# The first k quad of an attention-plus-MLP kernel: loaded in f16 by GpSimd's casting DMA instead of an f32 load and a VectorE cast

## The chip, the core and the metric

The kernel runs on one core of one Trainium2 chip. The core has five engines that run side by side, each with its own list of instructions that it takes strictly in order: TensorE (PE in the profile, with its weight loads shown as PEld), VectorE (DVE), ScalarE (ACT), GpSimd (POOL) and SyncE (SP). [...] Transfers between HBM and the on-chip memory SBUF are done by 16 DMA engines; a DMA is issued from the list of one engine, here SP (queue q1 in the profile) or POOL (queue q0). Matrix products land in PSUM, which has eight banks, P0 to P7.

The metric is the device time in microseconds of one execution. Before the change the median of three runs is 365.93 us (365.68 to 366.21).

## The reference

Two stages. The first is an attention without softmax: for 8 batches and 12 heads, with 448 positions and a head size of 64,

```
scores = q @ k.T / sqrt(64)
attn   = max(scores, 0)**2 / 448
out    = attn @ v
```

The result, reshaped to 3584 tokens of 768 values, goes through two dense layers with a sigmoid GELU between them:

```
h = x @ w_in                              # 768 -> 2048
g = h / (1 + exp(-1.702 * h))
y = g @ w_out                             # 2048 -> 768
```

All inputs and the output are f32 in HBM. The kernel computes in f16 with f32 accumulation.

## The kernel before

**Tiles.** The attention is cut into 24 quads, numbered 0 to 23: one batch and four of its heads. For each quad there is a tile of q, of k and of v, each 128 partitions x 2 x 448 values. A quad's 448 keys are cut into 7 chunks j of 64. For a chunk, `scores` (line 143) makes four small products into two PSUM banks, one bank for each of the two head pairs a = 0 and 1. `relu` (line 156) copies one bank to SBUF through a max with 0, on ScalarE by default or on VectorE; `square` (line 165) squares a chunk; `attn_v` (line 173) multiplies with v. Before the scores, q and k have to be f16 and transposed. In the first quads this is done on TensorE: `trans_pe` (line 126) transposes into a PSUM bank with 14 small matmuls, and `trans_evac` (line 136) copies the bank to SBUF on VectorE. The dense layers then run over blocks of 384 and 512 tokens, as soon as the attention of those tokens is done.

**Two ways to load.** `load` (line 97) is an f32 DMA from SP into a staging tile, `kst` or `qst`, of which there is one each; `cast` (line 107) then makes the f16 tile on the engine that its word names. `load_cast` (line 102) is one DMA from POOL that reads f32 and writes f16. Both end in a tile of the pools `k16` and `q16`, two buffers each.

**What sets the order.** Nothing is planned at run time. A long list of words, written out by hand in line 468 and after, is turned into instructions one word after another, so each engine's list has the order of the words. The words that matter here, with u the quad:

- `jk`u, `jq`u: `load_cast` of k or q from POOL. `V`u: the same for v. `jwb2`: a part of w_in from POOL. `I`: the identity that the transposes need, made on POOL.
- `Lk`u, `Lq`u: `load` from SP. `K`u:d, `Q`u:a: the cast, on VectorE (d) or ScalarE (a).
- `z13@0 z1`: 14 matmuls of zeros on TensorE into bank P0.
- `tq`u@b, `tk`u@b: the transposes into bank b. `eq`u, `ek`u: their copies out of PSUM, on VectorE.
- `s`u.j@b.c: the scores of chunk j into banks b (a = 0) and c (a = 1). `r`u.j.a: the relu of one of the two banks, on ScalarE, or on VectorE with `:d`. `x`u.j: the square.

A bank is free again when the instruction that reads it is done. So a score waits for two readers, and TensorE, being in order, lets everything behind it wait too. The list begins like this (line 469; wrapped here):

```
jq1 z13@0 z1 jk1 I jwb2 Lq0 Q0:a tq0@1 Lk0 jq2 K0:d tk0@2 eq0 ek0 jk2 tq1@3 eq1
s0.2@4.5 s0.3@6.7 tk1@0 r0.2.1 V0 r0.3.0 r0.3.1:d ek1 r0.2.0 s0.5@1.2 r0.5.0
s0.1@3.5 r0.1.0:d s0.0@6.7 r0.0.0 r0.5.1:d r0.1.1 jk3 s0.4@0.4 s0.6@1.3 ...
```

Quad 0 alone has q and k loaded in f32 from SP; quads 1 to 5 use POOL's casting DMAs, and later quads use SP again with transposing DMAs.

Of the kernel before, what the change touches and what calls it, by code (L numbers as in the profile page):

```python
# [15 lines left out]
def kernel(  # L16
# [406 lines left out]
    with tc.manual_schedule():  # L423
# [35 lines left out]
        def zeros(e, p, n):  # L459
# [8 lines left out]
            "jq1 z13@0 z1 jk1 I jwb2 Lq0 Q0:a tq0@1 Lk0 jq2 K0:d tk0@2 eq0 ek0 jk2 tq1@3 eq1 "  # L468
            "s0.2@4.5 s0.3@6.7 tk1@0 r0.2.1 V0 r0.3.0 r0.3.1:d ek1 r0.2.0 s0.5@1.2 r0.5.0 s0.1@3.5 "
            "r0.1.0:d s0.0@6.7 r0.0.0 r0.5.1:d r0.1.1 jk3 s0.4@0.4 s0.6@1.3 r0.6.1:d r0.6.0 "  # L470
            "s1.0@6.2 r1.0.1 r1.0.0 r0.4.0 V1 r0.0.1:d s1.2@5.3 r0.4.1:d jq3 x0.6:a jwb0 r1.2.0 "
            "x0.5 s1.1@1.2 r1.1.1 x0.4 s1.5@6.0 r1.5.0:d x0.0 r1.5.1 jwa0 r1.2.1:d s1.3@7.4 x0.3 "
            "r1.1.0 x0.2 s1.4@5.2 x0.1:a tq2@6 x1.0 tk2@0 eq2 x1.5:a jk4 a0@3.1 ek2 r1.3.0 e0.1.0 "
            "jq4 s1.6@6.0 V2 jwa2 tk3@7 x1.1:a e0.0.0 r1.4.0 jwb1 r1.4.1:d ek3 s2.0@3.5 x1.4 "
            "e0.0.1:a tq3@2 jwa1 r1.3.1 x1.3 r2.0.1 jk5 s2.4@7.4 r1.6.0 r2.4.0 jq5 V3 e0.1.1 "
            "r2.4.1:d jwb3 s2.1@5.6 x1.2 r1.6.1 x1.6 s2.2@7.1 r2.0.0 a1@4.0 jwa3 r2.2.1 V4 r2.1.0 "
            "r2.2.0 r2.1.1 V5 x2.0 e1.0.0:a eq3 e1.1.0 s2.6@3.1 e1.0.1:a x2.1 jo1.0 r2.6.0 e1.1.1 "
            "s2.3@5.7 s2.5@6.2 r2.3.0 r2.3.1:d x2.2 r2.5.1 jo0.0 f0.3.0@4 f0.3.1 r2.6.1:d s3.3@3.0 "
            "s3.2@5.7 r3.2.1:d r3.3.1 r3.3.0 tk4@2 r2.5.0:d tq4@1 x2.3:a ek4 jo1.1 r3.2.0 x2.4 "
            "f0.2.0@7 x2.5:a x2.6 f0.2.1 s3.0@0.3 a2@6.2 r3.0.1 e2.0.1:a e2.1.0:a eq4 s3.1@5.3 "  # L480
            "r3.1.0 e2.1.1:a e2.0.0 jo0.1 r3.1.1:d x3.1 f0.1.0@1 f0.1.1 f0.1.2 x3.2 f0.3.2 r3.0.0 "
            "f0.2.2 g0.1 g0.3 v0.3:d f0.0.0@5 v0.1:d g0.2 s3.5@2.6 s3.6@3.0 r3.6.0 s3.4@1.4 r3.6.1 "
            "r3.4.1 r3.4.0:d f0.8.0@7 f0.8.1 f0.0.1 r3.5.1 r3.5.0:d f0.0.2 x3.4 v0.2 f0.8.2 "
            "s4.2@3.0 g0.0 r4.2.1:d x3.3:a s4.3@4.1 s4.1@6.2 r4.1.1 x3.5 r4.1.0 f0.6.0@5 f0.6.1 "
            "r4.3.0 x3.0 f0.6.2 g0.6 f0.4.0@0 f0.4.1 f0.4.2 g0.8 r4.3.1:d r4.2.0:d s4.4@2.6 "
            "r4.4.0:d tk5@4 x3.6 r4.4.1 tq5@5 g0.4 v0.4 s4.0@7.1 eq5:a ek5 s4.5@3.2 G3 a3@6.0 "
            "s5.6@5.4 r4.5.1 r4.0.0:d r4.5.0 x4.4 x4.2:a e3.0.0 s5.0@2.7 f0.7.0@3 r5.0.1:d r5.6.0:d "
            "r5.0.0 Lk6 f0.7.1 x4.1:a f0.10.0@6 r4.0.1 Lq6 f0.10.1 f0.10.2 g0.10 v0.10 f0.5.0@7 "
            "f0.5.1 f0.5.2 g0.5 K6:p e3.0.1:a Lk7 f0.7.2 f0.11.0@5 v0.6:d f0.11.1 r5.6.1 s5.1@2.1 "
            "r5.1.0 s4.6@6.7 f0.11.2 r5.1.1 f0.15.0@0 r4.6.0 v0.0:d x4.0 f0.15.1 x4.3 f0.15.2 g0.7 "  # L490
            "r4.6.1:d s5.4@4.2 x4.5 r5.4.1 x4.6 a4@1.6 r5.4.0:d s5.5@3.7 g0.11 s5.3@2.4 g0.15 "
            "e4.0.1:a s5.2@5.0 v0.15 r5.5.1:d x5.0:a f0.13.0@6 f0.13.1 f0.13.2 r5.5.0:d r5.3.0 x5.4 "
            "Rk6 x5.5:a V6 f0.9.0@7 S3.1 v0.8 e4.0.0 f0.9.1 r5.3.1 f0.14.0@3 v0.5 f1.4.0@2 f0.9.2 "
            "S3.2 f0.14.1 f0.14.2 g0.13 v0.7 V8 g0.9 r5.2.0:d f0.12.0@1 f0.12.1 S0.1 f0.12.2 V7 "
            "f1.1.0@4 v0.9 r5.2.1 v0.11 f1.4.1 f1.7.0@6 g0.14 v0.14 x5.2 f1.7.1 x5.3:a u1.3.0@7 "
            "x5.6 T1.1 x5.1:a a5@5.0 f1.1.1 g0.12 t1.3.0 Q6:d S1.1 e5.0.1:a u1.2.0@3 S2.1 Lq8 S2.2 "
            "f1.0.0@1 e5.0.0:a f1.1.2 S2.4 v0.12:d t1.2.0 f1.4.2 S1.2 T1.2 v0.13 S2.3 Rq6 g1.4 T1.4 "
            "A0.0.1@0 u1.2.1@0 b1.2.1 W0.1 f1.0.1 f1.3.0@5 f1.3.1 f1.3.2 W2.1 A0.0.3 f1.2.0@2 S3.3 "
            "u1.3.2 g1.1 g1.2.1 v1.1 f1.5.0@4 f1.5.1 v1.2.1 K7 f1.2.1 g1.3 f1.2.2 Lk8 W1.1 g1.2 "
            "f1.5.2 S3.4 A0.0.2@1 f1.7.2 g1.5 v1.2:d u1.2.2 v1.3 g1.7 f1.0.2 g1.0 v1.5 v1.4 t1.2.2 "  # L500
            "f1.6.0@5 t1.3.2 f1.6.1 T1.3 p0.0.0@2 W3.1 v1.0:d f1.6.2 u1.2.4 Q8:a t1.2.4 W0.2 u1.2.3 "
            "h0.0.0 v1.7:d W2.2 u1.3.4 W0.3 b1.2.3 g1.6 u1.2.5 W2.3 v1.6:d Lq7 g1.2.3 v1.2.3 "
            "s6.0@4.6 r6.0.0 W1.2 s6.2@1.5 u1.2.6 u1.3.1@4 r6.2.0:d Rk7 W3.2 b1.3.1 r6.0.1 Rq8 W3.3 "
            "W1.3 g1.2.5 s6.1@1.6 p0.0.1@3 r6.1.0 W0.4 t1.3.4 x6.0:a g1.3.1 u1.3.5 u1.3.3 r6.1.1:d "
            "l0.0.1 r6.2.1 p0.0.2 b1.2.6 x6.2:a b1.3.3 Q7:a Rq7 h0.0.2:d s6.5@1.6 r6.5.0:d r6.5.1 "
            "v1.3.1 s6.3@5.0 r6.3.1:d g1.3.5 K8:p x6.1:a v1.3.5 Lq9 Q9 u1.3.6 b1.3.6 g1.3.6 v1.3.6 "
            "Lk9 K9:p p0.0.4 h0.0.4 s6.4@1.6 r6.4.1 W3.4 r6.3.0 W2.4 r6.4.0 s6.6@0.7 r6.6.0 W1.4 "
            "A0.0.4 v1.2.5 p0.0.3 r6.6.1:d p0.0.5 x6.4 x6.5:a s7.2@4.6 l0.0.3 r7.2.0 r7.2.1 x6.3 "
            "Rk8 s7.0@5.1 r7.0.1:d r7.0.0 g1.2.6 l0.0.5 s7.1@0.7 r7.1.1:d p0.0.6 x6.6:a l0.0.6 Lq10 "
            "s7.3@4.6 A0.2.5@1 r7.1.0 r7.3.1 o0.1 r7.3.0:d a6@1.5 Lk11 e6.1.1 e6.1.0 e6.0.1:a "  # L510
            "s7.6@2.7 x7.2 r7.6.0 r7.6.1 Q10 e6.0.0:a s7.4@3.0 r7.4.0:d p1.0.0@6 s7.5@4.5 Rq9 "
            "r7.4.1 s8.1@2.7 r7.5.1 r8.1.0 s8.0@1.3 r8.0.1 x7.3 r7.5.0:d r8.0.0 x7.1:a Rk9 x7.6:a "
            "K11:p i0.2.0@0 s8.6@5.2 r8.6.0 x7.0 x7.5 r8.6.1 x8.6:a r8.1.1:d x7.4 n0.2.0 x8.1 "
            "a7@3.4 e7.1.0:a e7.0.0:a Lk10 Lq11 v1.2.6 s8.2@1.5 e7.1.1:a S1.4 s8.3@2.7 x8.0:a K10:p "
            "r8.2.0:d e7.0.1 A1.0.1@0 r8.2.1:d i0.2.1@0 r8.3.1 A1.0.3 r8.3.0 Rk11 A1.0.2@1 h1.0.0 "
            "n0.2.1:a p1.0.1@3 x8.3:a V9 o0.2 s8.4@1.4 s8.5@5.7 r8.4.0 r8.4.1 r8.5.1 x8.2 Q11 "
            "r8.5.0:d s9.2@2.0 Lk12 o0.0 V10 Rk10 r9.2.1:d V15 p1.0.2 x8.4 s9.1@1.4 r9.2.0 x8.5 "
            "s9.0@7.5 r9.1.0 a8@0.2 r9.1.1:d r9.0.0 s9.4@1.4 r9.0.1 s9.3@7.5 r9.3.1 l1.0.1 p1.0.3 "
            "e8.1.1:a u2.1.0@5 e8.0.1:a u2.0.0@2 S0.2 r9.3.0 S1.3 r9.4.1:d e8.0.0:a u2.1.1@7 t2.1.0 "
            "r9.4.0:d t2.0.0 T2.1 u2.2.0@4 e8.1.0 g1.3.3 T2.2 t2.2.0 T2.4 u2.0.2 T2.3 b2.1.1 "  # L520
            "u2.0.1@1 Lq12 g2.1.1 v1.3.3:d S0.3 u2.1.2 b2.0.1 u2.2.1@0 t2.0.2 t2.1.2 v2.1.1 g2.0.1 "
            "v2.0.1 u2.0.4 t2.0.4 A1.2.1@0 x9.1:a u2.1.4 u2.0.3 t2.1.4 u2.2.2 u2.1.3 S0.4 Rq11 "
            "b2.0.3 u2.0.6 g2.0.3 Rq10 b2.2.1 K12:p u2.0.5 b2.1.3 u2.1.6 g2.2.1 v2.2.1:d v2.0.3 "
            "g2.1.3 b2.0.6 u2.1.5 t2.2.2 v2.1.3:d Lk13 A1.0.4 u2.3.0@1 g2.0.5 b2.1.6 u2.2.4 "
            "t2.3.0:d g2.0.6 u2.3.1@2 g2.1.6 v2.0.5 b2.3.1 v2.0.6 u2.2.3 t2.2.4 g2.1.5 v2.1.6 "
            "g2.3.1 v2.1.5 b2.2.3 u2.3.2 t2.3.2 A1.2.2@1 x9.4:a h1.0.2:d u2.2.5 v2.3.1 u2.2.6 "
            "b2.2.6 u2.3.3 g2.2.5 Q12:a u2.3.4 p1.0.4 h1.0.4 v2.2.5 s9.5@7.5 g2.2.3 r9.5.0 g2.2.6 "
            "x9.3 t2.3.4:d s9.6@0.4 b2.3.3 u2.3.5 g2.3.5 u2.3.6 r9.5.1:d r9.6.1 K13:p p1.0.5 "
            "r9.6.0:d l1.0.3 Rk12 b2.3.6 x9.2 Lk15 l1.0.5 s10.3@7.1 r10.3.1 V13 K15:p s10.1@5.4 "
            "s10.0@0.2 r10.0.1 Rq12 p1.0.6 x9.6 r10.3.0:d r10.0.0 x10.0 r10.1.0 p1.2.0@6 r10.1.1:d "  # L530
            "x9.0:a l1.0.6 g2.3.6 h1.2.0 x9.5 s10.5@1.2 s11.1@7.0 r11.1.1 a9@5.4 r10.5.1 r10.5.0:d "
            "v2.2.6:d Lq14 o1.0 r11.1.0 A1.2.3 s10.2@3.0 s10.6@2.1 v2.3.5 r10.6.0 r10.2.0 r10.2.1 "
            "r10.6.1:d p1.2.1@7 e9.0.0 x10.3:a p1.2.2 s11.0@2.3 e9.0.1:a Q14 l1.2.1 o1.1 r11.0.1 "
            "s10.4@0.1 s11.3@5.4 x10.6 Lq13 A1.2.4 r11.0.0:d p1.2.3 r10.4.1 x10.1 h1.2.2 p1.2.4 "
            "r11.3.1 x10.5 r10.4.0 r11.3.0 x10.4 x10.2:a h1.2.4:d x11.3 l1.2.3 s11.2@3.2 x11.1 "
            "r11.2.0 r11.2.1 x11.2 Lk14 s12.2@1.4 v2.3.6 a10@0.5 s11.5@3.2 r12.2.0 r11.5.1 Rk13 "
            "Rq14 p1.2.6 e10.0.0 r12.2.1 x11.0:a r11.5.0:d l1.2.6 v2.2.3:d e10.0.1:a g2.3.3 "
# [133 lines left out]
```

## Time and profile before

| what | value |
|---|---|
| median of three runs | 365.93 us |
| the profiled execution's own time | 365.47 us |
| its span, first to last instruction | 363.7 us |
| TensorE busy | 355.3 us (98%) |
| VectorE busy | 309.6 us (85%) |
| ScalarE busy | 283.2 us (78%) |
| GpSimd busy | 123.4 us (34%) |
| moved by DMA | 51.39 MB |
| first scores of quad 0 start | 7.50 us |
| TensorE in the first 5 us | 3.84 us busy, all of it zeros |

The time is what the runs report; the span lies inside it, and the 1.8 us between the two are before the first and after the last instruction. A row of the timeline gives the start and the busy time in microseconds, the engine, the line, what is written from what, and how many instructions are merged in it; the brackets at the end tell how long the engine sat idle before and which work released it. A busy TensorE is not a TensorE at its peak, since the ends of matmuls are modelled.

### The profile page before, as it was taken

How to read it: one execution, taken by the hardware profiler on the slowest of the kernel's cores; microseconds unless marked ns; L12 is line 12 of the kernel's file. 1: busy time of each engine (PE TensorE's matmuls, PEld its weight loads, DVE VectorE, ACT ScalarE, POOL GpSimd, SP SyncE). 2: the span in 40 equal slices, each digit the busy share in tenths (PEclk: the TensorE clock that was granted, in tenths of full speed). 3: DMA queues.
4: the chain of work that ended last, by engine and by line, in shares of the span. 5: the costliest groups of instructions: out<-in, count | busy, mean ns of one | idle time of the engine just before them, and what ended most of it. 6: DMA issues, size and time to landing. Idle time of an engine off the chain costs nothing.

```text
span 363.7 us, 9020 instructions
## 1 busy us (share of the span) xinstructions
PE 355.3 (98%) x3562; PEld 231.8 (64%) x3562; DVE 309.6 (85%) x577; ACT 283.2 (78%) x550; POOL 123.4 (34%) x171
## 2 busy tenths in 40 slices
PE   8899999999999999999999999999999999999995
PEld 4445555655579555885569655787558755687763
DVE  3998999799899998988999799978897999775672
ACT  3998995799989888988997899588996598362410
POOL 5655174425526240254243251145202221021300
PEclk9999999999999999999999999999999999999999
DMA  8999999959898789458995599515590031110315
GB/s 193 188 205 205 238 230 203 203 57 268 178 219 171 136 254 172 135 103 187 195 193 114 126 186 213 133 51 104 99 198 8 1 88 43 45 45 2 87 36 141
DMA packets 65227, 51.39 MB, mean 141 GB/s; under 512 B 35744, under 2 KB 61856, under 8 KB 65184
## 3 DMA queue, kind: packets, MB, share of 16 engines
q1 hardware_dynamic: 48256, 36.32, 42.3%
q0 software_dynamic: 16608, 14.09, 26.1%
q8 instruction: 28, 0.46, 0.5%
q10 hardware_dynamic: 320, 0.39, 0.3%
q14 instruction: 15, 0.12, 0.1%
HBM read 45.61 MB, written 11.01 MB: 156 GB/s over the span
## 4 chain that ended last, share of the span: by engine, by line
PE 87%; ACT 5%; DVE 5%; DMA 1%; issue 1%; SPq 0%; ACTq 0%
PE ox L203 29%; PE hx L203 29%; PE sc L150 9%; PE av L181 8%; PE ht L228 7%; PE os L203 4%; ACT at L163 3%; DVE at L161 1%; DMA kst<-in_k_dram 1%; ACT at L169 1%; DVE at L88 1%; ACT xe L79 1%; DVE asum L88 1%; PE tr L131 1%; DVE xe L83 0%
## 5 line engine op out<-in xcount | busy, mean ns | idle before, releaser
L163 ACT ACTIVATE at<-sc 128x448 f16<-128x448 f32 x228 | 111.5, 574 | 13.6 <-PE sc L150 12.2
L169 ACT ACTIVATE at<-at 128x896 f16<-128x896 f16 x72 | 68.6, 967 | 0.4
L161 DVE TENSOR_SCALAR at<-sc 128x448 f16<-128x448 f32 x108 | 64.4, 615 | 5.1 <-PE sc L150 4.6
L88 DVE TENSOR_TENSOR at<-at 128x896 f16<-128x896 f16 x96 | 61.4, 657 | 3.2 <-ACT at L163 2.7
L203 PEld LDWEIGHTS <-win 128*128 128x128 f16 x624 | 56.7, 98 | 8.6 <-issue 2.4
L217 POOL TENSOR_SCALAR go<-gf 128x512 f16<-128x512 f32 x48 | 35.9, 747 | 71.2 <-ACT gf L214 57.5
L88 DVE TENSOR_TENSOR gf<-hx,gf 128x512 f32<-128x512 f32 (+1 forms) x78 | 47.7, 624 | 14.3 <-PE hx L203 9.6
L214 ACT ACTIVATE gf<-gf 128x512 f32<-128x512 f32 (+1 forms) x78 | 44.5, 581 | 15.2 <-DVE gf L88 15.0
L150 PE MATMUL sc<-qT,kT 64*64 64x448 f16 x672 | 51.7, 359 | 1.7 <-ACT at L163 0.7
L217 POOL TENSOR_SCALAR ge<-gf 128x384 f16<-128x384 f32 x47 | 29.4, 626 | 65.7 <-ACT gf L214 63.7
L203 PE MATMUL ox<-wout,go 128*128 128x384 f16 x256 | 46.1, 326 | 0.0
L203 PEld LDWEIGHTS <-winS 128*128 128x128 f16 x468 | 42.5, 98 | 5.5 <-issue 1.6
L203 PEld LDWEIGHTS <-go 128*128 128x128 f16 x320 | 30.1, 98 | 22.4 <-issue 4.8
L181 PE MATMUL av<-at,v 64*64 64x448 f16 x672 | 36.6, 350 | 0.3
L203 PE MATMUL hx<-T,winS 128*128 128x256 f16 (+1 forms) x312 | 36.8, 260 | 0.0
L203 PEld LDWEIGHTS <-ge 128*128 128x128 f16 x256 | 24.2, 98 | 17.4 <-issue 3.4
L150 PEld LDWEIGHTS <-kT 64*64 64x64 f16 x672 | 18.0, 105 | 26.8 <-issue 21.5
L203 PE MATMUL ox<-wT,asum 128*128 128x384 f16 x192 | 34.9, 326 | 0.0
L79 ACT ACTIVATE gf<-hx 128x512 f32<-128x512 f32 (+1 forms) x50 | 26.3, 542 | 11.0 <-PE hx L203 7.6
L203 PE MATMUL hx<-xo,win 128*128 128x256 f16 x252 | 32.1, 273 | 0.0
L203 PEld LDWEIGHTS <-asum 128*128 128x128 f16 x224 | 21.2, 98 | 16.1 <-issue 2.3
L181 PEld LDWEIGHTS <-v 64*64 64x64 f16 x672 | 20.5, 107 | 11.9 <-issue 2.1
(77 smaller groups left out, 472.7 us busy)
## 6 DMA issues: line engine op xcount, KB each, us to landing
out_dram<-osb SPq DMA_DIRECT2D x52, 192.0 KB, 3.1
qst<-in_q_dram SPq DMA_DIRECT2D x19, 448.0 KB, 4.1
kst<-in_k_dram SPq DMA_DIRECT2D x19, 448.0 KB, 5.0
v<-in_v_dram POOLq DMA_DIRECT2D x24, 224.0 KB, 6.3
win<-in_moe_w_in_dram POOLq DMA_DIRECT2D x8, 384.0 KB, 10.7
wout<-in_moe_w_out_dram POOLq DMA_DIRECT2D x4, 768.0 KB, 22.3
q<-in_q_dram POOLq DMA_DIRECT2D x5, 224.0 KB, 7.6
k<-in_k_dram POOLq DMA_DIRECT2D x5, 224.0 KB, 6.7
```

The costliest lines, as they stand in the source:

```text
L79: nc.scalar.activation(out=o, in_=i, func=AF.Copy)
L88: eng[e].tensor_tensor(out=o, in0=x, in1=y, op=op)
L131: nc.tensor.matmul(out=ps[64 * a:64 * a + 64, j * 128:(j + 1) * 128], lhsT=x[:, a, 64 * j:64 * j + 64], rhs=ident[:, :], is_transpose=True)
L150: nc.tensor.matmul(out=sc[a][c, 0:S], lhsT=st["kT"][r, j, c], rhs=st["qT"][r, :, c], start=True, stop=True)
L161: nc.vector.tensor_scalar(out=o, in0=i, scalar1=0.0, scalar2=None, op0=ALU.max)
L163: nc.scalar.activation(out=o, in_=i, func=AF.Relu)
L169: nc.scalar.activation(out=at, in_=at, func=AF.Square)
L181: nc.tensor.matmul(out=av[s][64 * a:64 * a + 64, 0:S], lhsT=v16[r, a, 64 * j:64 * j + 64], rhs=at[r, a, :], start=(j == 0), stop=(j == J - 1))
L203: nc.tensor.matmul(out=o, lhsT=lhs(i), rhs=rhs(i), start=start and i == 0, stop=i == n - 1, skip_group_check=True)
L214: nc.scalar.activation(out=o, in_=i, func=AF.Gelu_apprx_sigmoid, scale=1.0 / SC)
L217: eng[e].tensor_scalar(out=o, in0=i, scalar1=SC, scalar2=1.0, op0=ALU.mult, op1=ALU.mult)
L228: nc.tensor.matmul(out=hp[g, f][:, 0:n], lhsT=w[:, i, fo:fo + 128], rhs=xts[g][:, i, 0:n], start=i == 0, stop=i == NK - 1)
```

## The change

Quad 0's k no longer comes as `Lk0` and `K0:d`. It comes as `jk0`, a casting DMA, and that is the first instruction that POOL issues. The list of words is also put in another order in its first stretch; after `r0.2.0` it is the same, word for word, to its end.

```diff
-jq1 z13@0 z1 jk1 I jwb2 Lq0 Q0:a tq0@1 Lk0 jq2 K0:d tk0@2 eq0 ek0 jk2
-tq1@3 eq1 s0.2@4.5 s0.3@6.7 tk1@0 r0.2.1 V0 r0.3.0 r0.3.1:d ek1 r0.2.0
+jk0 jq1 z13@0 z1 I jk1 jwb2 Lq0 Q0:a tq0@1 jq2 tk0@2 eq0 ek0 jk2
+s0.2@4.5 s0.3@6.7 r0.2.1 tq1@3 tk1@0 V0 r0.3.0 r0.3.1:d eq1 ek1 r0.2.0
 s0.5@1.2 r0.5.0 s0.1@3.5 r0.1.0:d s0.0@6.7 r0.0.0 r0.5.1:d r0.1.1 jk3 ...
```

Engine by engine:

- POOL: before jq1, jk1, I, jwb2, jq2, jk2; after jk0, jq1, I, jk1, jwb2, jq2, jk2. One DMA more, and jk1 behind the identity.
- SP: before Lq0, Lk0; after Lq0 alone. The next k load from SP is Lk6, much later.
- VectorE: before K0, eq0, ek0, eq1, r0.3.1, ek1, r0.1.0; after eq0, ek0, r0.3.1, eq1, ek1, r0.1.0. The cast is gone, and eq1 stands behind r0.3.1.
- TensorE: before tq0, tk0, tq1, s0.2, s0.3, tk1, s0.5; after tq0, tk0, s0.2, s0.3, tq1, tk1, s0.5.
- ScalarE: the same.

The functions are untouched: `load_cast` was there for quads 1 to 5, and its k and q take turns in the same two buffers as before.

## The prediction

> **What bounds the kernel now.** I read the shares of busy time first: TensorE 98%, so over most of the span TensorE sets the time. But the change touches none of that work: the list is the same after `r0.2.0`. So it can only move the moment at which the rest begins. The chain of work that ended last begins with the load of quad 0's k, to 5.49 us, then its cast, its transposes, the copy of kT, the first scores, and from 7.93 us ScalarE's relus. That stretch in the timeline (start, busy us, engine, line, work; in brackets the idle time before, and what ended it):
>
> ```profile
> 4.31 0.95 ACT L79 ACTIVATE q<-qst 128x896 f16<-128x896 f32 x1 [2.07 <-DMA qst<-in_q_dram]
> 5.31 0.58 PE L131 MATMUL tr<-ident,q 128*64 128x128 f16 x14
> 5.51 0.63 DVE L83 CAST k<-kst 128x896 f16<-128x896 f32 x1 [4.41 <-DMA kst<-in_k_dram]
> 6.06 0.62 DVE L83 COPY qT<-tr 128x896 f16<-128x896 f16 x1
> 6.19 0.58 PE L131 MATMUL tr<-ident,k 128*64 128x128 f16 x14 [0.30 <-DVE k L83]
> 6.45 0.71 POOL L104 DMA_DIRECT2D q<-in_q_dram  x1 [2.36 <-DVE k L83]
> 6.61 0.56 PE L131 MATMUL tr<-ident,q 128*64 128x128 f16 x14
> 6.82 0.62 DVE L83 COPY kT<-tr 128x896 f16<-128x896 f16 x1
> 7.36 0.61 DVE L83 COPY qT<-tr 128x896 f16<-128x896 f16 x1
> 7.50 0.57 PE L150 MATMUL sc<-qT,kT 64*64 64x448 f16 x8 [0.33 <-DVE kT L83]
> 7.93 4.47 ACT L163 ACTIVATE at<-sc 128x448 f16<-128x448 f32 x10 [2.67 <-PE sc L150]
> 8.00 0.58 PE L131 MATMUL tr<-ident,k 128*64 128x128 f16 x14
> 8.15 0.62 DVE L161 TENSOR_SCALAR at<-sc 128x448 f16<-128x448 f32 x1 [0.17 <-PE sc L150]
> 8.51 4.51 PE L150 MATMUL sc<-qT,kT 64*64 64x448 f16 x40
> 8.69 0.61 DVE L83 COPY kT<-tr 128x896 f16<-128x896 f16 x1
> 9.22 2.80 DVE L161 TENSOR_SCALAR at<-sc 128x448 f16<-128x448 f32 x5
> ```
>
> Two things to see. The cast stands on the way to the first scores, and holds back the copy of qT too, which was ready when tq0 ended at 5.89. And once ScalarE starts at 7.93 it runs without a gap. The busy times by stretch (columns: stretch, length, then busy us of PE, PEld, DVE, ACT, POOL, with counts, clock, DMA share, GB/s) say how long that lasts:
>
> ```profile
> 10.00:12.50 2.50, 2.26 (x21) 0.78 (x20) 2.50 (x6) 2.50 (x7) 2.34 (x4) 1.00 1.18 158
> 12.50:15.00 2.50, 1.71 (x31) 0.84 (x32) 2.50 (x6) 2.50 (x6) 0.00 (x0) 1.00 1.23 191
> 15.00:20.00 5.00, 4.81 (x85) 2.70 (x80) 5.00 (x11) 5.00 (x10) 4.14 (x6) 1.00 1.25 205
> ```
>
> DVE and ACT are both full to 20 us. TensorE waits for none of its transfers between 14 and 60 us, and is 100% busy from 35 us. So a shift of both engines' streams at 10 us should reach the end nearly whole.
>
> Last, the DMA queues in slices of 0.2 us, at 4.4, 4.6 and 4.8 us (packets, MB, share of 16 engines):
>
> ```profile
> q1 hardware_dynamic: 45, 0.08, 104.1%
> ...
> q1 hardware_dynamic: 45, 0.08, 98.0%
> q0 software_dynamic: 3, 0.00, 8.2%
> ...
> q0 software_dynamic: 36, 0.03, 98.6%
> q1 hardware_dynamic: 21, 0.02, 24.2%
> ```
>
> POOL's first transfer, jq1, was issued at 1.25 us, yet q0 moves nothing until q1, with q and k of quad 0, runs dry.
>
> [...] Here SP's first DMA moved packets 1.1 us after its issue, and a lone v load at 246.0 us moved its first at 1.4 us and landed at 3.7[...]. [...] jq2, which needs tq0 (over at 5.89), began at 6.45, 0.31 after the cast's end at 6.14. [...] the longest new idle time below is 0.85 us, so I leave the clock alone.
>
> **The change part by part.** Two groups: the new load, and the new order.
>
> *Is jk0 in time?* It takes jq1's place: issued at 1.25, first packet not before 2.65 (1.25 + 1.4). Before, q1 carried 512 packets to 5.0 us at 225 a us. Now it carries q's 256, which end at about 3.7. Then jk0's 256 packets at q0's rate (47 in 0.2 us, 235 a us) take 1.1 us, to 4.8; jq1 itself took 1.7 us from its first packet (4.75) to landing (6.45), so jk0 should land at about 5.4. It is needed when tq0 has gone through: tq0 starts at 5.31 as before (it waits for ScalarE's cast of q and the end of the zeros), and a following set of transposes enters 0.42 later (6.19 to 6.61): 5.73. In time by 0.3. jq1 then lands at 6.5, as before. jk1, now issued after the identity at about 3.5, is ready by 4.9, before the engines reach it at 5.9, and lands at 7.65 as before (2.15 + 5.5). Total packets are the same, so the rest of the queue is unmoved. [...]
>
> *SP* loses one issue of 0.45 us, with nothing behind it until Lk6 at 37.94: nothing. *POOL* gains one issue of 0.7 us in a stretch where it then sat idle 2.36 us before jq2: nothing. Its buffer waits stay the same kind: jk2 waits for tk0 as before, jk3 for tk1, which ends at 8.66 instead of 8.58.
>
> *The first scores.* tk0 5.73, ends 6.31 (+0.58). VectorE: eq0 at 5.94 (5.89 + 0.05), ek0 0.54 later (6.82 to 7.36) at 6.48, done 7.10. s0.2 at 7.16 (before 7.50): **0.34 us gained**. The cast of 0.63 yields no more, because the path of q sets the start now, and the two copies stand one behind the other.
>
> *What the order does with it.* s0.3 is 0.21 behind (8.51 to 8.72, the second four of that row) at 7.37. tq1 follows s0.2 by 0.50 (7.50 to 8.00 before, for tk1): 7.66, done 8.24. tk1 8.08, done 8.66. s0.5 follows by 0.51: 8.59 (before 8.51). VectorE sits idle from 7.10 to 7.81, when s0.3 is there (7.37 + 0.44), where before it did eq1. Then r0.3.1 at 7.81, eq1 at 8.35 to 8.97 (before 7.36 to 7.97), ek1 to 9.50. Now s0.1 needs bank P3, which eq1 empties: 9.02, before 8.72. Behind it in TensorE's order, s0.0 goes at 9.23, before 8.96. Relus come 0.43 after their scores:
>
> - ScalarE: r0.2.1 at 7.59 (0.34 early), two more at 0.42 each, r0.5.0 at 9.02 (s0.5; 0.20 early), r0.0.0 at 9.66 (before 9.64). The gain is gone.
> - VectorE: r0.1.0 at 9.45 (before 9.22), r0.5.1 at 9.98, done 10.59 (before 10.36).
> - s1.0's second bank is P2, freed by r0.5.1: 10.64, before 10.42. r1.0.1 on ScalarE then at 11.07; its own turn would be 9.66 + 3 x 0.42 = 10.92, and it was 10.91 before. **0.16 us lost**.
>
> Sum: -0.34 to the first scores, +0.50 by the later eq1 and what stands behind it: +0.16 from 11 us on, with VectorE at about +0.2. Both run full after that, so nothing gives it back before 20 us, and I find no slack that surely does later. The profiled execution would take 365.47 + 0.16 = 365.63. The median shown is 0.46 above that execution, so by the median 365.93 + 0.16 = **366.1 us**, which is no change: 0.2% of the time is 0.73 us, about what a measurement of this kernel can tell from none.
>
> **Rivals.**
>
> *The gain is kept.* If eq1 doesn't delay s0.1 (had VectorE a faster way to it, or the relus more slack than the 0.43 I use), ScalarE keeps its 0.34: 365.6. For it: ScalarE's first wait of 2.67 us is the chain. Against it: 0.71 us of new idle time on VectorE.
>
> *Absorbed.* Between 20 and 30 us VectorE is idle for 1.3 us and ScalarE for 0.6, so that a late stream can catch up there if TensorE isn't waiting for it just then: 365.9. Against it: TensorE also waits for both in that stretch (0.26 us for VectorE at 23.78).
>
> *jk0 is late, and the kernel slower.* If q0's first packet at 4.75 was not queueing but the start-up of POOL's first DMA (3.5 us after its issue), jk0 lands where jq1 did, at 6.45. tk0 starts at 6.5, kT is ready at 7.7, s0.2 goes at 7.79, 0.63 later than above, and all behind it: 0.16 + 0.63 = +0.8, 366.7. It begins to cost when jk0 lands after 5.7, and passes 0.2% at a landing of about 6.4. For it: the trace has no other first DMA. Against it: 1.4 us for a lone v load, and each slice shows q0 taking up what q1 leaves.
>
> *The change doesn't do what it says* is not among them: the cast and the f32 load are gone from the lists.
>
> **How the numbers follow.** Forecast 0.55; gain kept 0.17; absorbed 0.13; jk0 late 0.15. Only the last stands at the 0.2% line (366.66), and gets 0.10 beyond it; shifts that reappear larger in a later stage, which I can't work out, add 0.06 to slower and 0.08 to faster. So faster 0.08, same 0.76, slower 0.16. The range goes from the kept gain with 0.3 for the scatter of runs (365.3) to the late jk0 with 0.3 (367.0). The forecast alone: 365.8 to 366.5.
>
> **What would show it.** Right: s0.2 at about 7.16 and tk0 right behind tq0; r0.2.1 at 7.6, but r0.0.0 near 9.66 and r1.0.1 near 11.07; eq1 at 8.35 and idle time before r0.3.1 on VectorE; q0's packets from 3.7 us. Wrong: TensorE idle before tk0 with a DMA as the releaser (jk0 late), q's landing later than 4.3 (the two queues mix after all), a wait for jk1 before tk1, or the streams apart at 20 us by something other than +0.2.

## The result, and the profile after

The changed kernel takes 368.25 us (median of 4 runs, 367.94 to 369.15) where the kernel before takes 366.07 (4 runs, 365.68 to 366.63): a ratio of 1.0062, 95% interval 1.0040 to 1.0085. It is slower by about 2 us, where 366.1 and no change were forecast. The profiled execution took 367.94 us, with a span of 366.2 against 363.7.

The same stretch of the timeline as before the change (start, busy us, engine, line, work; in brackets the idle time before, and what ended it):

```profile
4.31 0.95 ACT L79 ACTIVATE q<-qst 128x896 f16<-128x896 f32 x1 [2.08 <-DMA qst<-in_q_dram]
5.74 0.87 PE L131 MATMUL tr<-ident,q 128*64 128x128 f16 x14
6.54 0.58 PE L131 MATMUL tr<-ident,k 128*64 128x128 f16 x14
6.66 0.62 DVE L83 COPY qT<-tr 128x896 f16<-128x896 f16 x1 [5.56 <-PE tr L131]
7.20 0.61 DVE L83 COPY kT<-tr 128x896 f16<-128x896 f16 x1
7.87 0.57 PE L150 MATMUL sc<-qT,kT 64*64 64x448 f16 x8 [0.74 <-DVE kT L83]
8.37 0.58 PE L131 MATMUL tr<-ident,q 128*64 128x128 f16 x14
8.52 0.62 DVE L161 TENSOR_SCALAR at<-sc 128x448 f16<-128x448 f32 x1 [0.70 <-PE sc L150]
9.06 0.61 DVE L83 COPY qT<-tr 128x896 f16<-128x896 f16 x1
```

The cast is gone, and VectorE idles 0.70 us before r0.3.1, as worked out. But the first scores start at 7.87, not at 7.16. In this execution TensorE was slow for longer: the 14 zeros took 4.66 us in place of 4.21, so tq0 started at 5.74 in place of 5.31, and its 14 transposes took 0.87 us in place of 0.58. That hides how late k is, which landed at 6.50; the experiments show it bare. The busy times by stretch (stretch, length, busy us of PE, PEld, DVE, ACT, POOL with counts, clock, DMA share, GB/s) say that VectorE and ScalarE are full again from 10 us on:

```profile
10.00:12.50 2.50, 2.14 (x28) 0.78 (x21) 2.50 (x6) 2.50 (x6) 2.50 (x4) 1.00 1.15 160
15.00:20.00 5.00, 4.71 (x95) 3.07 (x94) 5.00 (x12) 5.00 (x10) 3.47 (x6) 1.00 1.26 204
```

To see where the rest went, each instruction is matched with the same one of the kernel before, and their starts are subtracted. The table gives the shift in us against the profiled execution before: of ScalarE's first relu, of ScalarE's instructions at 10 to 11 us, and the middle one of all instructions in a later stretch. The tail is a length, from the start of VectorE's last instruction to the end of the span:

| execution | first relu | ScalarE at 10-11 us | 25-88 us | from 104 us | from 287 us | tail | span |
|---|---|---|---|---|---|---|---|
| kernel before | 0 | 0 | 0 | 0 | 0 | 4.04 | 363.7 |
| changed kernel | +0.37 | +0.75 | +0.81 | +1.48 | +1.24 | 5.27 | 366.2 |

So there are two losses in the changed kernel: 0.8 at the start, and 1.23 in the last 5 us, where the list of words is the same. The step near 100 us is scatter: in the twelve later profiles it lies between -0.5 and +0.7, mostly near +0.6, and it is +0.6 in the second profile of the kernel before, whose first profile was on the fast side there. The tail is not: in the profiles below it is 4.03 to 4.06 with the old load, as long as VectorE has no instruction fewer, and 5.24 to 5.50 with the new load, as long as nothing is added in its place.

The closing waits of SyncE say what the tail waits for (engine, line, what it waited for: us in total, times, longest). In the kernel before:

```profile
SPq L666 <- DMA out_dram<-osb: 1.4, 2, 0.9
```

In the changed kernel:

```profile
SPq L665 <- DMA out_dram<-osb: 2.4, 3, 1.7
```

It waits for the output transfers, and longer. The DMA queues around the last outputs (packets, MB, share of 16 engines), first before, in the 1.0 us from 358.0, 1.65 us ahead of VectorE's last instruction:

```profile
q1 hardware_dynamic: 44, 0.05, 19.2%
q14 instruction: 1, 0.01, 2.8%
```

Then after, in the 1.0 us from 362.6, 1.71 us behind the start of that instruction, and in the 0.8 us behind it:

```profile
q1 hardware_dynamic: 77, 0.10, 42.8%
q10 hardware_dynamic: 75, 0.09, 25.9%
q14 instruction: 1, 0.01, 4.7%
...
q1 hardware_dynamic: 3, 0.00, 2.8%
q10 hardware_dynamic: 5, 0.01, 2.1%
```

One packet of 8 KB of instructions (0.047 x 16 x 1.0 = 0.75 us on one DMA engine) has moved from ahead of the last outputs into the midst of them. The packet runs from 1.87 to 2.62 us behind the start of VectorE's last instruction. Nearly all outputs are through by 2.63; four data packets of SP's queue (q1) and four of ScalarE's (q10) follow one behind the other from 2.62 to 3.32, by their spacing one engine's share (an estimate). Before, nothing comes after 2.63. The late share starts where the instruction packet ends in the other executions too: at 2.59 behind a packet that ends at 2.60 in the changed kernel repeated, and at 2.66 behind 2.67 in its third execution.

### The profile page after: what moved, and what is told of

Its sections match the earlier page's. It is cut to its first block, busy times and chain, and to the rows that moved or that the text cites. A ratio compares the mean times of both kernels' runs of the same rounds, so it can differ in the third digit from the quotient of the medians.

```text
span 366.2 us, 9018 instructions
## 1 busy us (share of the span) xinstructions
PE 355.8 (97%) x3562; PEld 232.1 (63%) x3562; DVE 309.9 (85%) x576; ACT 284.1 (78%) x550; POOL 123.8 (34%) x172
## 4 chain that ended last, share of the span: by engine, by line
PE 89%; DVE 5%; ACT 4%; issue 1%
PE hx L203 29%; PE ox L203 29%; PE sc L150 9%; PE av L181 7%; PE ht L228 7%; PE os L203 5%; ACT at L163 3%; DVE at L161 1%; PE zp L463 1%; DVE at L88 1%; PE tr L131 1%; DVE asum L88 1%; ACT at L169 1%; ACT xe L79 1%; DVE osb L396 0%
## 5 line engine op out<-in xcount | busy, mean ns | idle before, releaser
L88 DVE TENSOR_TENSOR at<-at 128x896 f16<-128x896 f16 x96 | 62.7, 671 | 3.4 <-ACT at L163 2.7
L214 ACT ACTIVATE gf<-gf 128x512 f32<-128x512 f32 (+1 forms) x78 | 44.6, 583 | 14.9 <-DVE gf L88 14.7
```

The costliest lines, as they stand in the source:

```text
L88: eng[e].tensor_tensor(out=o, in0=x, in1=y, op=op)
L214: nc.scalar.activation(out=o, in_=i, func=AF.Gelu_apprx_sigmoid, scale=1.0 / SC)
```

## The experiments

### Which part costs what: four kernels on one chip

*The changed kernel again, and the kernel before again*, unedited.

> The changed kernel once more, for a second profile. In the first one it lost 0.37 us up to the first scores [...], 0.5 by 20 us from the later eq1, 0.67 at 98 to 102 us where VectorE's additions met GpSimd's casts, and about 1.2 after the last output DMA was issued. Theory ORDER (only the later eq1 belongs to the change, the rest is scatter of single executions): the same 0.5 between first scores and 20 us, but the other three terms differ from the first profile; the ratio to before over the rounds is about 1.001 to 1.002. Theory SYSTEMATIC (all of it belongs to the change): ratio about 1.006, first scores again near 7.87 us, and the same loss at 98 to 102 us.

> The kernel before, unchanged, for a second profile. ORDER: first scores may lie anywhere between 7.5 and 8.2 us[...]; VectorE's two long additions at 98 to 101 us vary in length. SYSTEMATIC: first scores at 7.50, r0.0.0 at 9.64, the span 363.7 within 0.3. Ratio 1.000 in both.

*The load alone*: the casting load first on POOL, the rest of the list in its old order.

```diff
-jq1 z13@0 z1 jk1 I jwb2 Lq0 Q0:a tq0@1 Lk0 jq2 K0:d tk0@2 eq0 ek0 jk2
+jk0 jq1 z13@0 z1 I jk1 jwb2 Lq0 Q0:a tq0@1 jq2 tk0@2 eq0 ek0 jk2
 tq1@3 eq1 s0.2@4.5 s0.3@6.7 tk1@0 r0.2.1 V0 r0.3.0 r0.3.1:d ek1 r0.2.0
```

> The new load alone: jk0 first in POOL's queue and no f32 load or cast of k, but the old order of tq1, eq1 and the scores. ORDER: first scores 0.34 us earlier than before at the same clock, the relus all 0.3 earlier, ratio about 0.999. SYSTEMATIC, with the load as its cause [...]: ratio about 1.003 to 1.006, first scores near 7.9.

*The order alone*: the f32 load and the cast as before, the new order behind them.

```diff
 jq1 z13@0 z1 jk1 I jwb2 Lq0 Q0:a tq0@1 Lk0 jq2 K0:d tk0@2 eq0 ek0 jk2
-tq1@3 eq1 s0.2@4.5 s0.3@6.7 tk1@0 r0.2.1 V0 r0.3.0 r0.3.1:d ek1 r0.2.0
+s0.2@4.5 s0.3@6.7 r0.2.1 tq1@3 tk1@0 V0 r0.3.0 r0.3.1:d eq1 ek1 r0.2.0
```

> The new order alone: tq1 behind the first scores and eq1 behind r0.3.1, with the old f32 load and cast of quad 0's k. ORDER: first scores at 7.50 as before, r0.0.0 and r0.1.0 then 0.4 to 0.6 later than before, ratio about 1.0015. SYSTEMATIC with the order as its cause [...]: ratio about 1.004 to 1.006.

Measured, with the kernel before at 366.36 us (37 runs):

| kernel | us | ratio, 95% interval | first relu | ScalarE at 10-11 us | 25-88 us | from 104 us | from 287 us | tail |
|---|---|---|---|---|---|---|---|---|
| changed, again | 367.94 | 1.0036, 1.0020-1.0052 | +0.49 | +1.09 | +1.13 | +0.81 | +0.56 | 5.38 |
| before, again | 366.36 | 0.9999, 0.9986-1.0012 | +0.03 | +0.04 | +0.08 | +0.67 | +0.67 | 4.04 |
| load alone | 368.12 | 1.0040, 1.0025-1.0054 | +0.73 | +0.80 | +1.57 | +2.27 | +2.07 | 5.26 |
| order alone | 366.69 | 1.0006, 0.9994-1.0018 | +0.02 | +0.40 | +0.44 | +1.03 | +1.03 | 4.06 |

Neither theory holds as a whole: the repeated changed kernel loses again at the start and in the tail (SYSTEMATIC), but not near 100 us, where only scatter is seen (ORDER). By the times, the load carries the loss, and the order alone can't be told from no change. Within its execution the order costs 0.42 (+0.02 at the first relu, +0.44 from 25 us on), at the place that was worked out. Its timeline:

```profile
7.52 0.57 PE L150 MATMUL sc<-qT,kT 64*64 64x448 f16 x8 [0.72 <-DVE kT L83]
8.17 0.62 DVE L161 TENSOR_SCALAR at<-sc 128x448 f16<-128x448 f32 x1 [0.70 <-PE sc L150]
8.71 0.61 DVE L83 COPY qT<-tr 128x896 f16<-128x896 f16 x1
9.80 2.28 DVE L161 TENSOR_SCALAR at<-sc 128x448 f16<-128x448 f32 x4
```

eq1 (8.71) stands behind the relu of s0.3, and r0.1.0 comes at 9.80. The load shows two things. First, TensorE waits for k. In the changed kernel, repeated:

```profile
6.68 0.58 PE L131 MATMUL tr<-ident,k 128*64 128x128 f16 x14 [0.85 <-DMA k<-in_k_dram]
7.99 0.57 PE L150 MATMUL sc<-qT,kT 64*64 64x448 f16 x8 [0.72 <-DVE kT L83]
```

With the load alone:

```profile
6.59 0.58 PE L131 MATMUL tr<-ident,k 128*64 128x128 f16 x14 [0.76 <-DMA k<-in_k_dram]
7.72 0.58 PE L131 MATMUL tr<-ident,q 128*64 128x128 f16 x14 [0.55 <-DMA q<-in_q_dram]
```

There jq1 is waited for as well, since tq1 stands ahead of the first scores: the new load needs the new order. Second, the long tail belongs to the load, not to the order. The load alone also loses 0.77 between 11 and 25 us, where the granted clock is half from 14.9 to 18.3 us; more of that below.

### Why jk0 is late: three kernels on one chip

Issued at 1.25 us, jk0 landed 5.3 us later, at 6.50. In the kernel before, jq1 had the same place in the queue, moved its packets more than 1 us later, and landed at nearly the same time (profile after, then before; KB, us from issue to landing):

```profile
k<-in_k_dram POOLq DMA_DIRECT2D x1, 224.0 KB, 5.3
...
q<-in_q_dram POOLq DMA_DIRECT2D x1, 224.0 KB, 5.2
```

It wasn't the queue's start: q0 takes up what q1 leaves, from 3.6 us on (slices of 0.2 us at 3.6, 3.8 and 5.0 us, profile after):

```profile
q1 hardware_dynamic: 38, 0.05, 65.5%
q0 software_dynamic: 14, 0.01, 38.2%
...
q0 software_dynamic: 39, 0.03, 135.1%
q1 hardware_dynamic: 6, 0.00, 3.7%
...
q0 software_dynamic: 29, 0.03, 94.3%
```

The trace has 16 packets of 4 bytes for each of these transfers, taken here as the ends of the 16 DMA engines' shares; the semaphore of the transfer rises 16 times, and TensorE starts on the 16th. For jq1 before the change, all 16 packets came between 5.87 and 6.16 us. For jk0 in the changed kernel 13 came between 4.78 and 5.04, the others at 5.46, 5.86 and 6.05; repeated, 12 by 4.98, then 5.44, 5.64, 5.73 and 5.82. The 16th rise came at 6.50 and 6.64. Meanwhile 20 to 30 of q0's packets took over 0.1 us, the longest 0.57 and 0.81, in place of 0.088. It isn't the loading of instructions: no packet of an instruction queue moves from the start to 11.8 us in any profile. Three theories, with one edit each.

EARLY START (some engines lag when the queue starts as early as here, at 3.4 to 3.7 us): an unused f32 load of another quad's k from SP, behind that of q, holds q0 back to 4.75 us, when it started before the change.

```diff
-... I jk1 jwb2 Lq0 Q0:a tq0@1 jq2 ...
+... I jk1 jwb2 Lq0 X23 Q0:a tq0@1 jq2 ...      # X: load("k", 23), not used
```

> The changed kernel with one more f32 load from SP right behind q of quad 0: k of quad 23 into the free staging tile, which nobody reads (448 KB of work added, no result changed). The casting queue then begins at about 4.75 us as before the change, not at 3.5. Theory EARLY START [...]: no slow packets, jk0's 16 completions between 5.85 and 6.2 us, landing at 6.5, so first scores no later than in the changed kernel although 448 KB more were moved; jq1 lands at 7.6 as k1 did before. Theory FIRST TOUCH (the slow packets belong to these reads of k and q themselves, whenever they come): again a quarter of the engines 0.5 to 1 us behind, jk0 lands at about 7.7.

WRITING (GpSimd is busy issuing jk1 and jwb2 meanwhile, from 3.39 to 4.79 us in the repeated changed kernel): they are held behind a copy of two values on GpSimd that waits for ScalarE's cast of q.

```diff
-... I jk1 jwb2 Lq0 Q0:a tq0@1 jq2 ...
+... I Lq0 Q0:a P jk1 jwb2 tq0@1 jq2 ...        # P: gpsimd copy of q16[:, 0, 0:2]
```

> The changed kernel with jk1 and the part of w_in held back on GpSimd until ScalarE has cast q of quad 0 (a copy of two values on GpSimd waits for it), at 5.3 us[...]. Theory WRITING [...]: no slow packets in jk0, its completions between 4.75 and 5.05, landing at 5.5, TensorE does not wait for it and the first scores are near 7.2 at the fast clock. Theory EARLY START or FIRST TOUCH: jk0's last completions stay at 5.8 to 6.1 and it lands at 6.5. In all theories jk1 is late, by about 1 us, and so tk1.

FIRST TOUCH (it is k's data): jq1 goes first.

```diff
-jk0 jq1 z13@0 ...
+jq1 jk0 z13@0 ...
```

> The changed kernel with jq1 ahead of jk0 on GpSimd, so that quad 0's k is the second casting transfer. EARLY START: the first transfer, now jq1, has three or so late engines at 5.5 to 6.0 us; jk0 follows on each engine, last completion near 7.1, landing 7.5, first scores near 8.6 to 8.9, and the relus after them 0.6 to 0.9 us later than in the changed kernel. FIRST TOUCH of k: jq1 complete by 5.05, jk0 with late engines of its own.

Measured, with the kernel before at 366.11 us (7 runs); the last two columns are of the transfer that is first in the queue:

| kernel | us | ratio, 95% interval | first scores | engines' ends | landed |
|---|---|---|---|---|---|
| extra load | 368.01 | 1.0051, 1.0031-1.0071 | 7.90 | 5.86 to 6.18, none late | 6.48 |
| GpSimd quiet | 368.17 | 1.0056, 1.0037-1.0076 | 7.85 | two late, at 5.84 and 5.98 | 6.50 |
| jq1 first | 370.82 | 1.0131, 1.0110-1.0151 | 8.98 | 4.75 to 5.02, two late at 5.44 and 5.89 | 6.49 |

FIRST TOUCH falls, since the late engines go with the place in the queue, not with k. WRITING falls: GpSimd issues no DMA from 2.86 to 5.36 us, and a packet still took 1.13 us. EARLY START is the one left standing: with 448 KB more to move ahead of it, jk0 lands no later than without (6.48 against 6.50 and 6.64), and none of its packets takes longer than 0.088 us. What makes an engine lag inside an early queue wasn't settled. In the last kernel, k is really late:

```profile
7.68 0.58 PE L131 MATMUL tr<-ident,k 128*64 128x128 f16 x14 [1.56 <-DMA k<-in_k_dram]
```

Its 4.7 us aren't the price of that wait alone: the granted clock is half from 8.7 to 12.1 us, just behind it, and the mean clock of all four runs (0.990 to 0.995) is as low.

### The tail: five kernels, on two chips

The removed cast is one instruction less on VectorE. If the moved packet carries VectorE's instructions, a filler must move it back, and taking an unrelated instruction away must move it in the kernel before. The fillers write 1x1 constants that nothing reads.

```diff
 nc.vector.memset(warm, 0.0)
+nc.vector.memset(pad, 0.0)          # changed kernel, one more
```

> The changed kernel with one more instruction on VectorE: a memset of a 1x1 constant that nothing reads, at 0.9 us, where VectorE waits for nothing and nobody waits for it (0.06 us). It gives VectorE as many instructions as the kernel before has. All profiles with the new load have the end 5.3 us after the last VectorE instruction starts, all with the old load 4.0 us. INSTRUCTION FETCH (VectorE's instructions come by 8 KB transfers, and the removed cast moves each of these one instruction later, the last one from 1.4 us before that last instruction to 1.9 us after it, among the last outputs): the tail is back at 4.0 to 4.1 us, no output packet of the last two transfers comes after +2.7 us, VectorE's 0.30 us of issue near 282 us is back; time 367.1 (368.1 less 1.25, plus 0.24). NEW QUEUE (the tail belongs to the casting load, by its additional transfer in GpSimd's queue): the tail stays at 5.3, time 368.1.

```diff
-nc.vector.memset(warm, 0.0)         # kernel before, one fewer
-nc.scalar.activation(out=warm, in_=warm, func=AF.Gelu_apprx_sigmoid)
 nc.vector.memset(zero, 0.0)
+nc.scalar.activation(out=warm, in_=zero[0:1, 0:1], func=AF.Gelu_apprx_sigmoid)
```

> The kernel before, with its old load, cast and order, less one VectorE instruction: the memset of the 1x1 constant that warms ScalarE's table (0.06 us at 0.80 us) is gone, and that activation reads one element of the zero tile, which VectorE fills at 0.88 to 1.10 us in both, in its place; it starts at 2.03 us anyway, after the table's load. INSTRUCTION FETCH: the tail goes from 4.05 to 5.3 us, one engine's last output packets come after +3 us, and VectorE's 0.30 us of issue near 282 us is gone: time 366.36 plus 1.0, 367.4. NEW QUEUE: nothing changes, 366.4.

```diff
 nc.vector.memset(warm, 0.0)
+nc.vector.memset(pad, 0.0)          # kernel before, two more
+nc.vector.memset(pad2, 0.0)
```

> The kernel before with two more 1x1 memsets on VectorE at 0.9 us (0.12 us where it is idle). INSTRUCTION FETCH: the fetches come two instructions earlier; the tail stays at 4.0 to 4.1 us, and the stop near 282 us falls into a wait for TensorE of 0.22 us, so that up to 0.2 us of the 0.30 is hidden: 366.2, not told from 366.36 by the times, but seen in the trace. NEW QUEUE: 366.4, and the 0.30 us of issue at 282 us stays where it is.

These left 0.4 us of the tail, a stop between SyncE's closing waits. The next kernel fills SyncE too, and the changed kernel ran beside it.

```diff
 nc.vector.memset(warm, 0.0)
+nc.vector.memset(pad, 0.0)
...
-... s9.2@2.0 Lk12 o0.0 ...
+... s9.2@2.0 Lk12 Z0 Z1 o0.0 ...     # Z: SyncE loads one element of q
```

> The changed kernel with as many instructions on VectorE and on SyncE as the kernel before: the 1x1 memset on VectorE at 0.9 us, and on SyncE two loads of one element of q each, into constants that nothing reads, behind the load of k's quad 12. With VectorE alone filled the tail (from the start of VectorE's last instruction to the end of the span) was 4.43 us: the late output packets (0.75) were gone, but SyncE stood still for 0.38 us between its last waits, as in every profile with the new load and in none with the old load. SYNC'S FETCH (SyncE has the same stops in its own instructions, and the removed load moves one out of the wait for the last output, where it costs nothing, to behind it): the tail is 4.05 us, without late packets and without the stop between the closing waits; the start stays as in the changed kernel (first scores near 7.9 us, 0.8 to 1.1 us behind at 25 us); time 0.7 to 1.2 us below the changed kernel on the same chip, and still 0.5 to 1.0 us above the kernel before. NEW QUEUE (the 0.38 us are the wait for the additional transfer in GpSimd's queue): 4.43 us, as before this edit.

> The changed kernel as it is, on the same chip as the filled one. Both theories: tail 5.2 to 5.4 us, one engine's last output packets after +3 us, the stop of 0.38 us between SyncE's closing waits; time 368.0 where the kernel before takes 366.3. The difference to the filled kernel is the measure of what the moved fetches cost in the time.

Measured. The kernel before took 366.40 us (34 runs) beside the first three, 366.22 (26 runs) beside the last two. The instruction packet and the last end of an output are given from the start of VectorE's last instruction:

| kernel | us | ratio, 95% interval | instruction packet at | last output end | tail |
|---|---|---|---|---|---|
| changed, VectorE one more | 367.68 | 1.0035, 1.0020-1.0050 | -1.17 | +2.60 | 4.45 |
| before, VectorE one fewer | 367.08 | 1.0022, 1.0006-1.0038 | +1.96 | +3.10 | 4.78 |
| before, VectorE two more | 366.53 | 1.0004, 0.9994-1.0014 | -1.49 | +2.61 | 4.03 |
| changed, VectorE and SyncE filled | 366.85 | 1.0024, 1.0010-1.0037 | -1.37 | +2.60 | 4.03 |
| changed | 368.47 | 1.0065, 1.0044-1.0085 | +2.36 | +3.50 | 5.45 |

The packet is VectorE's: one instruction more or less on that engine, at 0.9 us where it idles, moves it at 360 us from ahead of the last outputs to among them, and back. Taking away a memset of 0.06 us made the kernel before slower by 0.7 us. SyncE's part is seen in the starts of its last waits (us from the same point; "->" marks a pause in which the transfers waited for had ended):

```
kernel before                 2.04   3.00 3.08 3.14
before, VectorE one fewer     2.02   3.71 3.79 3.86
changed, VectorE one more     2.02   2.98 3.05 3.12 -> 3.50
changed                       2.04   3.79 3.86 3.93 -> 4.32
changed, extra load on SyncE  2.04   3.95 -> 4.34 4.42
both filled                   2.01   3.05 3.12
```

The pause of 0.38 us stands one wait earlier where SyncE has one instruction more (the extra load of the second group), and is gone with both fillers, as if hidden in a wait for an output. The count of SyncE's list, with its waits, fits: 213 in the changed kernel, 214 with the extra load, 215 before, 217 with both fillers. A stop that moves one place ahead for each added instruction falls, in the kernel before, into the wait from 2.04 to 3.00, and with both fillers into an earlier one that ends at 1.73. So it goes with SyncE's own instructions, and the additional transfer in GpSimd's queue, which all the new-load kernels have, costs nothing at the end. The two parts add up: 4.04 + 0.39 = 4.43 with VectorE filled (4.45 found), 4.04 + 0.72 = 4.76 with VectorE alone moved (4.78). The forecast of 5.3 for the latter counted SyncE's part to VectorE.

SyncE's waits for the outputs in the kernel with both filled are back at the length of the kernel before:

```profile
SPq L669 <- DMA out_dram<-osb: 1.5, 3, 1.0
```

In time, the fillers bring 368.47 down to 366.85 on the same chip, 1.6 us, where the two profiles' tails differ by 1.42. With VectorE alone filled, 367.1 was forecast and 367.68 measured; its interval overlaps the changed kernel's, and only the trace shows that gain.

VectorE stops at another such place. In the kernel before, near 282 us:

```profile
281.38 0.56 DVE L88 TENSOR_TENSOR gf<-hx,gf 128x384 f32<-128x384 f32 x1
282.24 1.02 DVE L83 COPY gf<-hx 128x384 f32<-128x384 f32 x2 [0.30 <-issue]
```

and in the changed kernel:

```profile
282.86 0.56 DVE L88 TENSOR_TENSOR gf<-hx,gf 128x384 f32<-128x384 f32 x1
283.37 1.02 DVE L83 COPY gf<-hx 128x384 f32<-128x384 f32 x2
```

The engine waits for nothing, and an 8 KB instruction packet follows 0.7 us after the stop. This is the -0.24 at 287 us. The stop came back with one VectorE instruction more in the changed kernel, and went with one fewer in the kernel before (where the shift changed by only 0.05). With two more in the kernel before it moved ahead of the TENSOR_TENSOR before these copies, and the time didn't change. It is absent with both engines filled.

The count of VectorE's list, with its waits and from 0, fits all of these. The stop stands before number 575. That is the first of the two copies in the kernel before and with VectorE filled; the second, behind one that still runs, in the changed kernel and with one fewer; that TENSOR_TENSOR with two more. With both engines filled the list has one wait more by then, and number 575 is a wait for TensorE, in which the stop could be hidden. The trace has 28 packets of 16 KB in another instruction queue, one for each 254 of TensorE's 7124 matmuls and weight loads if those packets are TensorE's; by that estimate 8 KB are about 128 instructions. 128 on from 575, number 703 follows right behind VectorE's last computing instruction in the kernel before, and is the closing wait after that in the changed kernel, which fits the move of the last packet.

None of these kernels is faster than the kernel before.

## Why the prediction was wrong

**The start of q0: right.** Its first packets came in the slice at 3.6 us, as q1 ran out, where they had come in the one at 4.6; the start-up that the late rival assumed isn't there.

**jk0 "in time by 0.3": this step failed.** Its sum took one rate for all engines, 4.8 for the last packet and a landing at 5.4. 12 to 14 of 16 engines kept to it; the last came at 5.8 to 6.05, and jk0 landed 0.4 to 0.9 us behind that (0.3 for jq1 before), at 6.50 to 6.75: 1.1 to 1.4 us late. TensorE then waited 0.3 to 0.9 us for it, save in the first execution of the changed kernel, where tq0 itself lasted to 6.61. One execution is apart, and shows the rest of the step right. With VectorE filled, the last engine ended at 5.56 and jk0 landed at 5.87, the earliest of all:

```profile
5.19 0.58 PE L132 MATMUL tr<-ident,q 128*64 128x128 f16 x14
5.91 0.58 PE L132 MATMUL tr<-ident,k 128*64 128x128 f16 x14
7.22 0.57 PE L151 MATMUL sc<-qT,kT 64*64 64x448 f16 x8 [0.72 <-DVE kT L84]
```

First scores at 7.22, 0.28 early (0.34 forecast), and at 11 to 14 us ScalarE 0.24 and VectorE 0.29 late (0.16 and 0.2 forecast). Over seven executions of the new load in the new order with jk0 first, the first relu is +0.34 late in the mean (-0.28 to +0.60), over five with the old load +0.11 (-0.07 to +0.56): a loss of about 0.2, known roughly from so few, in place of a gain of 0.34. The rival "jk0 is late" had the place and nearly the landing (6.45), for a reason that isn't so.

**jk1 before tk1: wrong in part.** "The rest of the queue is unmoved" held on the average, not for the last engine: in the changed kernel's three executions jk1's last share ended at 8.46 to 8.91 in place of 7.30, and TensorE waited 0.26 us for it in the repeated one.

**jq2 behind the cast: this reading was wrong.** The prediction took jq2's start, 0.31 us behind the cast's end, as held back by the cast, which the profile before names as what released it. But in all executions save the one that keeps GpSimd quiet, jq2 starts 0.55 to 0.56 us behind the end of tq0, with the old load and with the new, which has no cast. In the changed kernel tq0 ends at 6.61:

```profile
7.17 0.70 POOL L104 DMA_DIRECT2D q<-in_q_dram  x1 [2.38 <-PE tr L131]
```

So the distance to the cast's end says nothing of a hold by the cast. The forecast doesn't rest on it.

**The order: right.** 0.50 forecast, 0.42 measured alone, by the mechanism named: eq1 behind r0.3.1, with 0.70 us of idle time before that relu. In the three executions of the changed kernel the same step, from the first relu to 14 us, is 0.42 to 0.64, with the wait for jk1 in it.

**The clock left alone: no difference between the loads is shown, but the reason failed.** The zeros ended at 4.97 us with GpSimd quiet and at 5.81 in the changed kernel, at 5.36 and 5.76 in two executions of the kernel before. So the start is known no better than these 0.4 us from one execution. The reason given was that the longest new idle time is 0.85 us; that this is too short to touch the clock was the author's estimate, and not shown. Three of the nine profiles with the new load show the granted clock halved, two of them behind shorter idle times: from 14.9 to 18.3 us with the load alone, from 14.4 to 17.8 with VectorE filled, from 8.7 to 12.1 with jq1 first. In the 3.4 us ahead, as long as the halved stretch itself, TensorE was busy for 2.31, 2.22 and 1.40 us, and idle for at most 0.70, 0.70 and 1.56 at a stretch. In the first two it cost 0.6 to 0.7 us. None of the five profiles with the old load shows it, but the mean clock of a run, 0.992 to 0.995 in these three profiles and 0.996 or more in the others, is at or below 0.995 in 23 of 104 runs of the kernel before and in 18 of 71 with the new load, jq1 first left out.

**SyncE's issue and VectorE's cast at no further cost: this step failed, and is the larger part.** The working counted what the removed instructions do, not that taking them away moves packets of instructions and stops at the other end of the kernel. "So it can only move the moment at which the rest begins" was wrong by this: from the start of the same last instruction on VectorE, the end came 1.23 us later. One instruction more or less on VectorE moved a packet of 8 KB; the stops took 0.30 us on VectorE and 0.38 on SyncE, and the outputs among which the packet came ended the wait for them 0.7 us later (3.71 against 3.00).

The sum by the terms: first scores +0.2 (forecast -0.34), order +0.42 (+0.50), near 282 us -0.24 (0), tail +1.2 to 1.4 (0): 1.6 to 1.8. Measured: 2.2, 1.6 and 2.2 in three comparisons. A halved clock, where it comes, isn't in this sum, nor is a step of 0.5 to 0.6 near 20 us in one execution of either load, which stays unexplained. Without the tail it is 0.4, and the kernel with both engines filled measured 0.63 (366.85 against 366.22; 0.4 to 1.4 by its interval). So with the instruction packets back in place the change is a small loss, at the upper end of the forecast's own range (366.5, 0.57 above the median of then), and not the gain that a shorter chain suggests.

## What to carry to other kernels

Where a small edit moves the time by more than its own chain can, match the two traces instruction by instruction and look for the step. Here one instruction less on VectorE moved a packet of instructions among the last outputs, and SyncE's shorter list went with a stop that no longer fell into a wait; the two cost 1.2 to 1.4 us together, and a filler of 0.06 us told the first of them apart. Count a transfer as landed with the last of its 16 engines: in seven of the eight executions in which the casting queue began early, its first transfer landed 1.1 to 1.4 us later than its mean rate had said.

## What was not expected of the hardware

- Instruction packets of 8 KB took 0.3 to 0.8 us near the end of the kernel, and 1.0 at 86 us in the changed one; where one came among the last outputs, the wait for them ended 0.7 to 1.0 us later (3.71 to 3.95 against 3.00). VectorE stood still for 0.30 us near 282 us in the kernel before, SyncE for 0.38 us between its closing waits in the changed one.
- Of a casting transfer that began at 3.4 to 3.7 us, 2 to 4 of 16 engines ended 0.3 to 1.0 us behind the others (5.46 to 6.05 against 5.04 in the changed kernel); of one that began at 4.6 to 4.8 us, none, with the old load (5.87 to 6.16) and with an extra load ahead (5.86 to 6.18).
- The 14 transposes of tq0 took 0.87 us in the changed kernel and 0.91 with the extra load, where they took 0.58 in the kernel before; 14 transposes took 0.96 at 14.77 us with VectorE filled, where the granted clock was half.
- With VectorE filled the granted clock fell to half for 3.4 us (14.4 to 17.8), though TensorE had been busy for 2.22 of the 3.4 us before, and idle for no more than 0.7 at a stretch.
